# Experts 4 to 7 in one pass over all their rows, in a Mamba-2 and switch-routing kernel

## The chip, the cores and the metric

The kernel runs on one core of one Trainium2 chip. The metric is the device time of one execution in microseconds, and the median of several executions is compared. Beside it there is one execution that the hardware profiler recorded; all durations of single instructions come from that one.

A core has a matrix engine (PE, with PEld for its weight loads), a vector engine (DVE), a scalar engine (ACT), GpSimd (POOL) and a sync engine (SP), which here only issues transfers. Each engine works through its own list of instructions in order; semaphores tie the lists together.

## The reference, cut to what matters

Two blocks stand one behind the other. The first is a Mamba-2 state-space scan over 4 batches, 8 heads, 768 positions, head dimension 32 and state size 16. Its result is turned into 3072 rows of 256 numbers. The second sends each row to one of eight experts:

```python
logits = x @ w_gate                      # 3072 x 8
expert_idx = np.argmax(logits, axis=1)
probs = softmax(logits)                  # the reference writes it out
gate_w = probs[np.arange(N), expert_idx]
for e in range(E):
    mask = expert_idx == e
    xe = x[mask]
    h = np.maximum(xe @ w1[e], 0.0)      # 256 -> 1024
    out[mask] = gate_w[mask, None] * (h @ w2[e])   # 1024 -> 256
```

How many rows an expert gets is known only once the scan and the routing are done. With the inputs of the reference the eight counts are 372, 343, 418, 417, 336, 365, 415 and 406.

## The kernel before, in words

**Attention part (0 to 60 us).** The scan is done in 12 steps `d`, each of two blocks of 128 positions (24 blocks `n`). A step loads its blocks (`load`, L183; the loop asks for blocks 2d+6 and 2d+7, so two to three steps ahead), masks and scales them (`masked_C` on ACT, `scaled_x` mostly on POOL), multiplies on PE (`scores`, `y_own`, `y_old`), applies the mask on DVE (`weigh`), carries the state on (`state`, `faded`, `whole`), and turns the result into rows together with their eight logits (`rows`, `rows_out`, `logits_of`). The order of all instructions is written out by hand in the main loop (`manual_schedule`, from L714); no planner moves them. The states of steps 4 and later need decay totals, which PE writes to PSUM in `totals` and `take_totals` (L248) copies out: `et` by DVE, `ew` by ACT (L252).

**Routing.** Blocks are grouped (`RGS`); for each group `choose`, `rank` and `ranked` find for every row its place in a table `x_hbm` in device memory, where expert `e` owns a stretch of `NR` rows, and `place` (L430; the DMA is at L421) writes the 128 rows of a block there with one indirect DMA issued by POOL. A row is `W` = 336 numbers (1344 bytes): the values, the parts of the logits, and the number of the token. Places that no token takes must hold zeros and a token number outside the output. Before the change this is done in two ways: `empty_last` (L174) writes zeros over the last 64 rows of the first 256 of each expert, at step 1 of the loop, before any row is placed; and `empty_rest` (L473) writes 128 rows behind the last row of each expert, once the counts are known, with eight indirect DMAs during the expert part.

**Expert part (60 us to the end).** Each expert's rows are worked on in two passes: a first pass over 256 rows, expert after expert (`m_h` and `m_y`, loop at L869), and a second pass over what is left, two experts at a time (`m_pair`, L615). "Up" is the multiplication by `w1`: eight tiles of 128 hidden values, two matmuls each, with the rows of the expert as moving columns (`up`, L547), and ACT takes each result through Relu into `hT` (L560 in the first pass, L628 in the second). "Down" is the multiplication by `w2`: here the hidden values are the stationary side, 128 rows of the expert to a tile, with eight matmuls of 256 columns for each tile (`m_y`, L586). The result is scaled by the gate value (`put`, by ACT at L573 or DVE at L571) and scattered to the output by POOL (L564).

The second pass has rows that are not known when the program is built, so it is a `Switch`: `SIZES` holds 17 numbers of columns from 128 to 192 in steps of four, DVE computes for each pair of experts which of them is the smallest that holds its rows (`over`, L447), PE and ACT load that number (`number_of`, L607) and branch into the case that has been built for it. A case holds both experts' up matmuls and, if there are more than 128 rows, one shared tile in which each expert owns 64 partitions (`m_half`, L592). A hint to fetch the case is given earlier (`switch_hint`). The end of the program holds a general path that is taken only if the routing does not fit these sizes.

**Buffers and queues.** `m_load` (L479) reads the rows of a pass back from `x_hbm` on SP's queue; `m_xT` (L515) transposes them on DVE and computes the gate values, with an exponential on ACT in between. Three `hT` buffers of 256 columns are used in turn. Weights of an expert are two matrices of 1 MB, each loaded in four parts of 256 KB by `load_w` (L202) on SP's queue. Experts 0 to 2 have memory of their own from the start; those of 3 to 7 lie in memory that the attention part has given back. Which step of the loop loads which part of the first weights stands in `wq` (L751): four parts at step 0, one each at steps 1 to 8, and four at step 9; the rest of expert 2 follows at step 10. All these are behind each other on SP: a transfer that waits holds up those issued after it.

Of the kernel before, what the change touches and what calls it, by code (L numbers as in the profile page):

```python
# [9 lines left out]
FP32 = mybir.dt.float32  # L10
BF16 = mybir.dt.bfloat16
I32 = mybir.dt.int32
# [22 lines left out]
W = RW + 16  # L35
# [4 lines left out]
SLACK, FEW = 64, 64  # L40
NR = N + 512
# [6 lines left out]
def ssd_then_moe(ctx, tc, xs_in, ae_in, wgx, w_gate, w1, w2, gx, gb, gc, ga, out):  # L48
# [35 lines left out]
    rest = route.tile([128, E], I32, name="rest")  # L84
    at_r = route.tile([128, E], FP32, name="at_r")
# [5 lines left out]
    steps = route.tile([1, len(SIZES) - 1], FP32, name="steps")  # L91
# [69 lines left out]
    def empty_consts():  # L161
# [4 lines left out]
        at_i = sm.tile([128, E], I32, name="at_i")  # L166
        nc.gpsimd.iota(at_i, pattern=[[NR, E]], base=0, channel_multiplier=1)
        nc.gpsimd.tensor_copy(at_r, at_i)
        steps_i = sm.tile([1, len(SIZES) - 1], I32, name="steps_i")
        nc.gpsimd.iota(steps_i, pattern=[[SIZES[1] - SIZES[0], len(SIZES) - 1]], base=P1 + SIZES[0],  # L170
                       channel_multiplier=0)
        nc.gpsimd.tensor_copy(steps, steps_i)

    def empty_last():  # L174

        x_e = x_hbm.rearrange("(e r) w -> r e w", e=E)
        nc.sync.dma_start(out=x_e[P1 - SLACK:P1], in_=bc(zrows[0:SLACK, None, :], [SLACK, E, W]))
# [70 lines left out]
    def take_totals(w):  # L248
# [3 lines left out]
        nc.scalar.copy(ew[:, 12 * w:12 * w + 12], p)  # L252
# [194 lines left out]
    def over():  # L447
# [3 lines left out]
        nc.vector.tensor_tensor(out=rest, in0=p[:, 0:E], in1=at_r, op=ALU.add)  # L451
# [6 lines left out]
        nc.vector.tensor_tensor(out=over_, in0=bc(most[:, :, None], sh), in1=bc(steps[:, None, :], sh), op=ALU.is_gt)  # L458
# [14 lines left out]
    def empty_rest(e):  # L473
        to_places(zrows[:, :], rest[:, e:e + 1])

    jobs = [(0, e) for e in range(E)] + [(1, e) for e in range(E)]
    ex = [dict() for _ in jobs]

    def m_load(i, engs=(nc.sync,)):  # L479

        p, e = jobs[i]
        r0, n = e * NR + P1 * p, (P1, P2)[p]
        xb = mo.tile([128, P1 // 32 * 64], FP32, name="xb", bufs=4)
# [4 lines left out]
        lt = mo.tile([128, 2, MID], FP32, name="lt", bufs=7)[:, 0:2 - p]  # L488
        nc.sync.dma_start(out=lt, in_=x_hbm[r0:r0 + 128 * (2 - p), DM:W].rearrange("(t p) w -> p t w", p=128))
        ex[i]["lt"] = lt  # L490
        if p and e % 2 == 0:
            lh = mo.tile([128, 1, MID], FP32, name="lh", bufs=3)
            for u in range(2):
                q = r0 + u * NR + 128
                nc.sync.dma_start(out=lh[64 * u:64 * u + 64, 0], in_=x_hbm[q:q + 64, DM:W])
            ex[i]["lh"] = ex[i + 1]["lh"] = lh

    def gates(mid, n):

        sh = [128, n, E]  # L500
        l = mo.tile([128, 2, E], FP32, name="t_l", bufs=2)[:, 0:n]
        logits(l, mid)
        mx = mo.tile([128, 2], FP32, name="t_mx", bufs=2)[:, 0:n]
# [489 lines left out]
```

## Time and profile before

| | us |
|---|---|
| median of three executions | 254.2 (253.08 to 256.35) |
| the profiled execution, its own time | 247.47 |
| its span, first to last instruction | 245.8 |
| busy: PE, PEld, DVE, ACT, POOL | 237.3, 201.3, 88.5, 92.7, 82.8 |
| up matmuls (L551), busy, 512 records | 90.0 |
| down matmuls (L586), busy, 384 records | 85.1 |
| moved by DMA | 39.75 MB |

A record of a matmul is half of one: each multiplication of 32-bit numbers is two instructions here, so 256 matmuls are 512 records. The length given for a single record includes time in which the next one is already running, so paces are taken from the starts of long groups. In a timeline line the first number is the start in us from the beginning of the span, the second the length of the group, then come engine, line, operation, what is written and read, and shapes; a bracket at the end gives the idle time before the group and what ended it. `PEldq` and `ACTq` are the sequencers of PE and ACT, which handle branches themselves and can be ahead of their engines.

### The profile page before, as it was taken

Reading aid. Unit: us, or ns where it says so; the run is one execution under the profiler, and the core shown is the slowest. Engines: PE = TensorE matmul, PEld = TensorE weight load, DVE = VectorE, ACT = ScalarE, POOL = GpSimd, SP = SyncE. Lnnn points to the kernel's source line nnn. Section 1 sums busy time; section 2 is a strip of 40 time slices with the busy share of each in tenths; the row PEclk is TensorE's granted clock in tenths of the full one; section 3 lists DMA queues with packets and bytes.
Section 4 is the critical chain, followed back from the end, with each engine's and each line's share of the span. In section 5 each row is a group of like instructions: output and inputs, shape, how many; then the busy total and the mean of one; then the engine's idle time right before and its main releaser. Section 6 shows DMA issues by size and latency. Waiting matters only on the chain. (4 is left out here: it accounts for less than half of the span.)

```text
span 245.8 us, 5525 instructions
## 1 busy us (share of the span) xinstructions
PE 237.3 (97%) x2021; PEld 201.3 (82%) x2021; DVE 88.5 (36%) x279; ACT 92.7 (38%) x312; POOL 82.8 (34%) x144
## 2 busy tenths in 40 slices
PE   8889899999999999999999999999999999999992
PEld 5567778777888888888888888888999969989781
DVE  4699879998520222020201102052316007040000
ACT  4656768981322224141422324131432502614200
POOL 2484688880038506060413330111113012013031
PEclk9999999999999999999999999999999999999999
DMA  6999979965932278696867779454303100001001
GB/s 174 327 328 323 332 250 302 291 263 102 274 141 97 112 144 274 189 256 217 235 243 213 272 168 311 87 99 82 73 13 68 32 15 29 27 4 40 3 16 45
DMA packets 36407, 39.75 MB, mean 162 GB/s; under 512 B 21947, under 2 KB 23806, under 8 KB 36352
## 3 DMA queue, kind: packets, MB, share of 16 engines
q1 hardware_dynamic: 32816, 30.24, 43.2%
q0 software_dynamic: 2880, 8.66, 9.3%
q8 instruction: 27, 0.44, 0.7%
q10 hardware_dynamic: 656, 0.18, 0.3%
q14 instruction: 28, 0.23, 0.3%
HBM read 29.72 MB, written 9.86 MB: 161 GB/s over the span
## 5 line engine op out<-in xcount | busy, mean ns | idle before, releaser
L551 PE MATMUL h_ps<-xT,w 128*128 128x256 f32 (+3 forms) x512 | 90.0, 334 | 0.3 <-ACT hT L628 0.3
L551 PEld LDWEIGHTS h_ps<-xT,w 128*128 128x128 f32 x512 | 80.8, 190 | 7.6 <-ACT hT L628 0.7
L586 PE MATMUL y_ps<-w,hT 128*128 128x256 f32 x384 | 85.1, 380 | 0.0
L586 PEld LDWEIGHTS y_ps<-w,hT 128*128 128x128 f32 x384 | 72.6, 190 | 10.5 <-issue 0.8
L564 POOL DMA_INDIRECT out_dram<-yo,lt x24 | 23.8, 991 | 58.1 <-DVE yo L571 31.3
L509 DVE TENSOR_REDUCE t_se<-t_sub 128x1 f32<-128x8 f32 (+1 forms) x20 | 3.3, 165 | 102.8 <-ACT t_sub L507 102.8
L560 ACT ACTIVATE hT<-h_ps 128x256 f32<-128x256 f32 x64 | 24.4, 384 | 29.4 <-PE h_ps L551 28.9
L282 DVE TENSOR_TENSOR M<-g,mask 128x1024 f32<-128x1024 f32 x24 | 28.2, 1218 | 3.8 <-PE g L277 3.6
L628 ACT ACTIVATE hT<-h_ps 128x128 f32<-128x128 f32 (+2 forms) x64 | 18.0, 292 | 24.1 <-PE h_ps L551 24.1
L421 POOL DMA_INDIRECT x_hbm<-rows,pos x24 | 23.9, 994 | 9.3 <-DVE pos L408 5.3
L573 ACT ACTIVATE yo<-y_ps,t_gt 128x256 f32<-128x256 f32 x14 | 6.6, 474 | 43.2 <-PE y_ps L586 43.2
L421 POOL DMA_INDIRECT x_hbm<-zrows,rest x8 | 7.7, 962 | 35.4 <-DMA lt<-x_hbm 24.9
L335 PE MATMUL y<-M,xp 128*32 128x128 f32 x384 | 15.3, 277 | 1.6 <-DVE M L282 1.3
L347 PEld LDWEIGHTS r<-turn,yT 128*128 128x128 f32 x88 | 12.2, 189 | 4.4 <-ACT yT L340 3.0
L261 ACT ACTIVATE cm<-xs_n,par 128x128 f32<-128x128 f32 x46 | 15.1, 419 | 1.5 <-DMA xs_n<-in_xs_dram 1.5
L347 PE MATMUL r<-turn,yT 128*128 128x160 f32 x88 | 14.9, 312 | 0.7 <-ACT ew L252 0.7
L564 POOL DMA_INDIRECT out_dram<-yh,lh x4 | 3.9, 983 | 33.1 <-ACT yh L602 21.2
L277 PE MATMUL g<-cm,xs_n 32*128 32x256 f32 x192 | 15.0, 423 | 0.0
L271 POOL TENSOR_TENSOR xp<-xs_n,Ei 128x256 f32<-128x256 f32 x20 | 12.1, 617 | 6.8 <-DVE last L241 3.6
L571 DVE TENSOR_SCALAR yo<-y_ps,t_gt 128x256 f32<-128x256 f32 x10 | 4.7, 483 | 24.2 <-PE y_ps L586 24.2
L340 ACT COPY yT<-y 128x512 f32<-128x512 f32 x12 | 7.0, 586 | 16.1 <-PE y L335 14.2
L520 DVE STREAM_TRANSPOSE xT<-xb 128x512 f32<-128x512 f32 (+1 forms) x16 | 9.8, 632 | 8.6 <-DMA xb<-x_hbm 7.1
(123 smaller groups left out, 156.2 us busy)
## 6 DMA issues: line engine op xcount, KB each, us to landing
w<-in_w_dram SPq DMA_DIRECT2D x64, 256.0 KB, 5.8
xs_n<-in_xs_dram SPq DMA_DIRECT2D x20, 320.0 KB, 5.8
xb<-x_hbm SPq DMA_DIRECT2D x30, 64.0 KB, 2.3
xb<-x_hbm SPq DMA_DIRECT2D x32, 48.0 KB, 2.4
xs_n<-in_xs_dram SPq DMA_DIRECT2D x4, 192.0 KB, 3.6
x_hbm<-zrows SPq DMA_DIRECT2D x1, 672.0 KB
lt<-x_hbm SPq DMA_DIRECT2D x8, 80.0 KB, 2.7
xs_n<-in_xs_dram SPq DMA_DIRECT2D x4, 128.0 KB, 2.3
```

The costliest lines, as they stand in the source:

```text
L261: nc.scalar.mul(t[:, u], st[n]["CT"], par[:, u:u + 1])
L271: eng.tensor_tensor(out=t, in0=st[n]["x"].rearrange("p (h d) -> p h d", d=D), in1=bc(Ei[:, n, :, None], [128, NH, D]), op=ALU.mult)
L277: nc.tensor.matmul(g_ps[:, q, n % 2], lhsT=st[n]["BT"][r], rhs=st[n]["cm"][r].rearrange("p u i -> p (u i)"), start=True, stop=True)
L282: nc.vector.tensor_tensor(out=t, in0=g_ps[:, :, n % 2].rearrange("p q (u i) -> p q u i", u=2), in1=bc(mask[:, None, None, :], [128, 4, 2, ...
L335: nc.tensor.matmul(y_ps[o:o + D, h // 4, CH * s:CH * s + CH], lhsT=st[n]["xp"][:, D * h:D * h + D], rhs=st[n]["M"][:, h], start=first, sto ...
L347: nc.tensor.matmul((to[s] if to else r_ps[:, s])[:, 256 * t:256 * t + 160], lhsT=sd[d]["yT"][:, t, CH * s:CH * s + CH], rhs=turn[:, t].rea ...
L421: s_ = nc.gpsimd.indirect_dma_start(out=x_hbm[:, :], out_offset=bass.IndirectOffsetOnAxis(ap=at, axis=0), in_=row, in_offset=None)
L551: nc.tensor.matmul(p[:, 0:n], lhsT=w[:, c:c + 128], rhs=xT[:, t, 0:n], start=(t == 0), stop=(t == KT - 1))
L560: nc.scalar.activation(ex[i]["hT"][:, f, 0:n], q, func=ACT.Relu)
L564: return nc.gpsimd.indirect_dma_start(out=out[:, :], out_offset=bass.IndirectOffsetOnAxis(ap=tok, axis=0), in_=yo[:, :], in_offset=None, b ...
L586: nc.tensor.matmul(p, lhsT=ex[i]["hT"][:, f, 128 * t:128 * t + 128], rhs=w_sb[e][1][:, f * DM:f * DM + DM], start=(f == 0), stop=(f == FT ...
L628: nc.scalar.activation(ex[i + u]["hT"][:, f, 0:n], q, func=ACT.Relu)
```

## The change

Seven things are changed together:

- Experts 4 to 7 no longer have a first pass. They have one pass over all their rows, two experts at a time, in the same `m_pair`, with their own list of sizes, `WSIZES`: 17 numbers of columns from 320 to 448 in steps of eight. A case holds both experts' up matmuls over all columns; three tiles of 128 rows each follow in `m_y`, and the shared tile holds rows from 384 on. Experts 0 to 3 keep their two passes, and the first-pass loop runs over four experts instead of eight.
- `hT` buffers have 448 columns, and there are two instead of three. Their columns 320 to 384 are filled with zeros by POOL at step 1.
- The rows of a one-pass expert are loaded into buffers of their own (`xw`, `xTw`, two each); the small buffers `lt` are three tiles wide and six instead of seven.
- All places that may stay empty are written with zeros at step 1 (`empty_places`): rows 192 to 255 of experts 0 and 1, and rows 320 to 447 of all eight, in two DMAs. `empty_rest` and its eight indirect DMAs are gone.
- Weights: the part loaded at step 1 moves to step 2 and so on, and step 9 loads one part instead of four; the other matrix of expert 1 is loaded at step 10 with all of expert 2. Experts 6 and 7 use the memory of experts 0 and 1, and their sixteen parts are issued after the first pair.
- In `take_totals`, the copy of `ew` for the second half of the steps is done by DVE instead of ACT.
- The case numbers of two pairs are loaded at a time; within a pair's turn the transposition of the next pair now stands before the loads of later ones in the text (they are on different engines).

```diff
+HE = E // 2
+PASS = ((0, P1, 2), (P1, P2, 1), (0, P1 + P2, 3))
+WSIZES = list(range(P1 + FEW, P1 + P2 + 1, 8))
...
+        for hT in hT_all:
+            nc.gpsimd.memset(hT[:, :, WSIZES[0]:P1 + 128], 0.0)
...
-    def empty_last():
+    def empty_places():
         x_e = x_hbm.rearrange("(e r) w -> r e w", e=E)
-        nc.sync.dma_start(out=x_e[P1 - SLACK:P1], in_=bc(zrows[0:SLACK, None, :], [SLACK, E, W]))
+        for r, n, e in ((P1 - SLACK, SLACK, 2), (P1 + FEW, P2 - FEW, E)):
+            nc.sync.dma_start(out=x_e[r:r + n, 0:e], in_=bc(zrows[0:n, None, :], [n, e, W]))
...
-        nc.scalar.copy(ew[:, 12 * w:12 * w + 12], p)
+        (nc.vector.tensor_copy if w else nc.scalar.copy)(ew[:, 12 * w:12 * w + 12], p)
...
-    def empty_rest(e):
-        to_places(zrows[:, :], rest[:, e:e + 1])
-
-    jobs = [(0, e) for e in range(E)] + [(1, e) for e in range(E)]
+    jobs = [(p, e) for p in range(2) for e in range(HE)] + [(2, e) for e in range(HE, E)]
...
-    hT_all = [mo.tile([128, FT, P1], FP32, name=f"hT{k}") for k in range(3)]
+    hT_all = [mo.tile([128, FT, P1 + P2], FP32, name=f"hT{k}") for k in range(2)]
...
     def m_half(i, n, yo):
-        e = jobs[i][1]
+        p, e = jobs[i]
+        a = 128 * PASS[p][2]
+        n = max(0, n - a)
...
     def m_pair(i, pp):
...
-            n = SIZES[c]
+            n = (SIZES, WSIZES)[p - 1][c]
...
-        wq = [0, 0, 0, 0, 1, 2, 3, 4, 5, 6, 7, 8, 9, 9, 9, 9]
+        wq = [0, 0, 0, 0, 2, 3, 4, 5, 6, 7, 8, 9]
...
-                for k in range(8):
-                    load_w(2, *divmod(k, 4))
+                for k in range(12, 24):
+                    load_w(k // 8, k % 8 // 4, k % 4)
...
-        for e in range(EW, E):
+        for e in range(EW, E - 2):
             w_sb.append([w2pool.tile([128, KT * F], FP32, name=f"w{u + 1}_{e}") for u in range(2)])
+        w_sb.extend(w_sb[0:2])
...
-        for i in range(E):
+        for i in range(HE):
...
-                if 1 <= i <= 4:
-                    for e in range(2 * i - 2, 2 * i):
-                        empty_rest(e)
                 m_load(i + 3)
-                if i == E - 1:
+                if i == HE - 1:
                     m_load(i + 4)
...
         for k in range(E // 2):
-            i = E + 2 * k
+            i = HE + 2 * k
             m_pair(i, pp)
             if k + 1 < E // 2:
                 tc.switch_hint(chosen(k + 1), len(SIZES), f"pair{k + 1}")
+                m_xT(i + 2)
                 for u in range(4, 6):
                     if i + u < len(jobs):
                         m_load(i + u)
-                m_xT(i + 2)
             m_y(i, pp)
             m_y(i + 1, pp)
+            if k == 0:
+                for e in range(E - 2, E):
+                    for j in range(8):
+                        load_w(e, *divmod(j, 4))
```

## The prediction

> **What bounds the kernel now.** I read the page's busy shares first, then TensorE's timeline from 85 us on, then who waits on TensorE, then the other engines' timelines in the attention part, and last the branches at the four pairs. PE is busy for 97% of the span. The Trainium skill warns that busy time flatters a pipelined engine, so I took the pace from the timeline instead (start, length, what, count):
>
> ```profile
> PE 237.3 (97%) x2021; PEld 201.3 (82%) x2021; DVE 88.5 (36%) x279; ACT 92.7 (38%) x312; POOL 82.8 (34%) x144
> ...
> 152.23 7.07 PE L586 MATMUL y_ps<-w,hT 128*128 128x256 f32 x32
> 159.14 7.07 PE L551 MATMUL h_ps<-xT,w 128*128 128x256 f32 x32
> 166.04 7.07 PE L586 MATMUL y_ps<-w,hT 128*128 128x256 f32 x32
> 172.95 7.31 PE L551 MATMUL h_ps<-xT,w 128*128 128x128 f32 x64
> 180.09 7.07 PE L586 MATMUL y_ps<-w,hT 128*128 128x256 f32 x32
> 187.00 9.25 PE L551 MATMUL h_ps<-xT,w 128*128 128x164 f32 x64
> ...
> 206.78 7.31 PE L551 MATMUL h_ps<-xT,w 128*128 128x128 f32 x64
> 213.92 7.07 PE L586 MATMUL y_ps<-w,hT 128*128 128x256 f32 x32
> 220.83 2.34 PE L551 MATMUL h_ps<-xT,w 128*128 128x160 f32 x16
> 223.44 6.79 PE L551 MATMUL h_ps<-xT,w 128*128 128x160 f32 x48 [0.27 <-ACT hT L628]
> ```
>
> From 60 us to the end each group starts where the last one ends; the only gap is 0.27 us. So the expert part is TensorE's own stream, and only its length counts. A matmul is two records. The pace by start times: 256 columns, 6.907 us for 32 records, 215.8 ns each; 128 columns, 7.14 for 64, 111.6; 164 columns (187.00 to 196.19), 143.6; 160 columns (223.44 to 230.16 for 48), 140.0. That is 2n/2.4 plus 2.5 to 7 ns: time goes with columns, and a record has little cost of its own.
>
> The attention part (to 60 us) is a ring of DVE, PE and POOL: DVE is busy 8.3 to 9.5 of every 10 us, DMA at a share of 0.97 to 1.01 from 10 to 30 us, POOL 8.5 of 10 from 30 to 50 us.
>
> The third reading is the branch into a pair's case (duration min/median/max in ns, then its start):
>
> ```profile
> L988 PEldq COMPARE_BRANCH  x1: 343/343/343, 169.4 to 169.4; - x1
> ...
> L988 PEldq COMPARE_BRANCH  x1: 3072/3072/3072, 183.6 to 183.6; - x1
> ...
> L988 PEldq COMPARE_BRANCH  x1: 3295/3295/3295, 217.2 to 217.2; - x1
> ```
>
> Into case 0 (128 columns) the branch takes 0.3 us; into case 9 (164) and 8 (160) it takes 3.1 and 3.3. PE's sequencer reaches it 3.4 to 3.6 us before the array runs out of work (183.6 against 187.00, 217.2 against 220.83). The long branch is hidden with about 0.3 us to spare.
>
> **What the Trainium skill says.** "TensorE: Matmul & The Clock Gate", Back-to-back issue gap: warm, N/2.4 + 2.5 ns. With two passes to a record the trace agrees at 256 columns (213.3 + 2.5). "Runtime: NRT & Kernel Launch", Instruction fetch mechanics: a taken branch outside what is prefetched must fetch its page by DMA first; the 0.3 against 3.1 us agrees. "DMA: Bandwidth & Descriptors", Queues, rings and completion order: an engine takes its queues in turn, packet by packet, so a fetch shares with data; no run here shows that price. "Perfetto Trace Analysis", Identifying the Most-Contended Engine, is the warning used above.
>
> **The change, part by part.** The reference's routing counts are 372, 343, 418, 417, 336, 365, 415, 406 rows. Pairs (0,1) and (2,3) keep 128 and 164 columns. Pair (4,5) takes 368 columns (case 6), pair (6,7) 416 (case 12).
>
> 1. *One pass.* Pair (4,5) now: two first passes of 6.907 and 7.14 us, together 20.95. After: 64 records of 368 columns at 736/2.4 + 2.5 = 309.2 ns, 19.79. Gain 1.16. Pair (6,7) now: 13.81 + 9.06 (9.33 less the 0.27 gap) = 22.87; after, 416 columns, 349.2 ns, 22.35. Gain 0.52. The down matmuls stay: three tiles for each expert before and after, the 32-row half too. The 0.27 gap goes: it stands because ACT, late from its own branch (first eviction at 223.08), had four h_ps buffers of 0.56 us in hand; wide ones are 1.24 to 1.40 each, some 5 us of cover. Sum −1.95. Evictions fall from 128 to 64 for experts 4 to 7; by 0.83 ns per column ((384 − 278)/128) a 416-column one takes about 0.52 us against 1.40: hidden. Hidden-state buffers drop from 3 to 2; each is refilled only after the down matmuls that read it, which PE has behind it, so nothing.
>
> 2. *Branches.* Pair (4,5) goes from case 0 (0.3 us) to case 6: between 0.3 and 3.3 us, against a lead of 3.4 to 3.6: 0 to 0.2. Pair (6,7): the same, 0 to 0.2. Pair (2,3) keeps case 9, but its branch (about 128 to 131 us) now meets the weights of part 3. If sharing adds nothing it is free; if it doubles 3.1 us, 2.8 of it show. ACT's branch (186.3 to 188.9, 2.6 us) is late beside it, over a cover of 2.3, and overlaps. I take +0.9 for all branches, 0 to +3; a gain is excluded, as none costs PE time now.
>
> 3. *Weights moved back.* Experts 6 and 7 (16 loads, 4 MB) go into the memory of 0 and 1: SP waits for pair (0,1)'s down matmuls, about 131 us, with nothing behind it but loads 10 and 11, first needed about 171. At 256 KB per 0.7 us (370 GB/s, as at 10 to 14 us) the data are in by about 138, needed at 192. Four loads leave the attention part for the burst at 60.8 us (12 instead of 8): +2.8 us, in by about 72; the second matrix of expert 1 is used at 83, expert 2 at 90. Covered. The eight writes of empty rows (7.7 us of POOL, 27.7 us of waits of SP's x loads) go; those waits ended before any PE wait, so nothing is gained. The x loads for the first pair move up instead: by my count of SP's issues they land by about 107, when DVE wants them; a microsecond of lateness would only hold evictions that PE needs after 112.
>
> 4. *Empty places in step two.* 1152 rows of 1344 B in two DMAs instead of 512 rows in one: 0.86 MB more, less one weight load moved off. At the 211 to 343 GB/s seen from 16 to 22 us that is 2.5 to 4.1 us, less 0.7: what is queued behind, the xs_n loads issued at 16.5 and 17.2 (7.0 us to landing), comes 1.8 to 3.4 us later, from 23.5–24.2 to 25.3–27.6. ACT reads them from 24.86, is done 1.3 us later, and then has 1.82 us idle before 28.44: 0 to 0.7 of delay. POOL's first placement (23.04) waits for these writes and holds the sums of states and xp behind it; POOL's idle after it is 0.85, 1.29 and 0.60 us up to 35.2, and xp made at 26.7 is used at 32.4: about nothing. POOL's two added fills of hT (512 elements each; 336 took 0.37 us) cost about 1.1, covered by its 2.60 idle at 20.11; without that cover they would add as much.
>
> 5. *Copy by VectorE.* PE waits 0.67 us at 30.15 for ACT's ew copy (0.22 us at 29.88, behind yT, Er, Ei and S). On DVE it follows its neighbour at about 28.1, costs 0.17 to 0.2 there, before an idle 0.42. Gain up to 0.67 for PE; but the first expert starts when its rows are placed and read, and POOL, which places them, has only 0.28 + 0.21 of waits after 37 us to give up. Parts 4 and 5 together: −0.2, from −0.67 to +0.8.
>
> Sum: −1.95 + 0.9 − 0.2 = −1.25. The profiled execution took 247.47 us (span 245.8): 246.2. The median shown, 254.2, lies 6.7 above that execution; its three runs span 253.08 to 256.35. I carry the difference over: 253.0.
>
> **The rivals.**
> *A, the branch shows.* The fetch into pair (2,3)'s case shares DMA with 3 MB of weights, and the wide cases lie far off. For: 0.3 us to spare, and case 0 is left. Against: other busy stretches show no PE gap, though there nothing branches. With 3 us at pair (2,3) and 0.4 at the wide pairs: −1.95 + 3.4 − 0.2 = +1.3, 255.5, slower than before. It decides once the added branch time exceeds 2.15 us.
> *B, the empty rows reach PE.* If placement and xs_n come later than POOL's and ACT's slack, the attention part grows by 1.8 us: −1.95 + 0.9 + 1.8 = +0.75, 255.0. For: DMA at 1.0 there. Against: three idle stretches of POOL, and loads issued two steps ahead.
> *C, everything hidden.* No branch shows, and the copy gives its 0.67: −2.6, 251.6.
>
> **How the numbers follow.** Forecast 0.5, A 0.2, B 0.12, C 0.18. Range 250.6 (C less 1 for the spread of medians) to 256.4 (A plus 0.9). A measurement here tells about 2% from no change: 249.1 and 259.3. Beyond the first I see only luck, 0.05; beyond the second a branch or a queue far worse than seen, 0.08; within, 0.87.
>
> **What would show it.** Right: up-projection groups of 64 records spaced about 309 and 349 ns, no gap in them; no wait of PE for ew; the first placement near 25 us; the start of the first expert at 60.0 to 60.6. Branch entries of 3 us or more for the wide pairs, and a gap of PE near 131. Wrong if the wide records take more than columns tell, if PE waits for late rows near 60 us, or if a branch costs many microseconds.

## The result and the profile after

The change made the kernel slower. The median is 265.35 us (262.31 to 268.28, six executions) against 254.22 us (253.08 to 256.35, six executions of the kernel before beside them). The ratio is 1.037, with a 95% interval of 1.032 to 1.042. This ratio leaves out the two longest of the six executions after, 268.13 and 268.28 us, which are 2.2% and more above the shortest; the profiled one (span 266.6) is one of the two, so its two losses below are checked in a second profile.

The page of the kernel after: busy times, and further down the granted TensorE clock in 40 slices.

```profile
PE 245.2 (92%) x1893; PEld 191.8 (72%) x1893; DVE 88.2 (33%) x260; ACT 83.6 (31%) x267; POOL 75.1 (28%) x129
...
PE   7897999897999999993999489999999999999992
...
PEclk9999899997999999998699979999999999999998
```

PE has 128 records fewer and yet is busy for 8 us more. Two slices of PE stand out at 3 and 4 tenths, in the middle of a part that was without gaps before. The clock row has a 6 behind the first of them and a 7 behind the second: the granted clock fell there. The timeline of PE in that stretch (start, length, what, count, idle before and who ended it):

```profile
112.15 7.07 PE L554 MATMUL h_ps<-xT,w 128*128 128x256 f32 x32
119.06 2.32 PE L589 MATMUL y_ps<-w,hT 128*128 128x256 f32 x10
125.42 7.88 PE L589 MATMUL y_ps<-w,hT 128*128 128x256 f32 x22 [4.05 <-DMA w<-in_w_dram]
133.14 7.31 PE L554 MATMUL h_ps<-xT,w 128*128 128x128 f32 x64
140.29 7.07 PE L589 MATMUL y_ps<-w,hT 128*128 128x256 f32 x32
149.50 2.49 PE L554 MATMUL h_ps<-xT,w 128*128 128x164 f32 x16 [2.14 <-DVE yo L574]
154.28 8.62 PE L554 MATMUL h_ps<-xT,w 128*128 128x164 f32 x48 [2.29 <-ACT hT L633]
...
173.43 19.95 PE L554 MATMUL h_ps<-xTw,w 128*128 128x368 f32 x64
193.22 7.07 PE L589 MATMUL y_ps<-w,hT 128*128 128x256 f32 x32
200.77 14.08 PE L589 MATMUL y_ps<-w,hT 128*128 128x256 f32 x64 [0.48 <-DVE yo L574]
214.69 22.51 PE L554 MATMUL h_ps<-xTw,w 128*128 128x416 f32 x64
```

The wide passes are as computed: from 173.43 to 193.22 is 19.79 us for 64 records of 368 columns; from 214.69 to 237.13, where the next group starts, is 22.44. What was lost stands ahead of them. The down matmuls of expert 3 take from 119.06 to 133.14, 14.08 us where 32 such records took 6.907. And the up matmuls of pair (2,3) begin 2.14 us late and stop again for 2.29 us.

**The first loss.** The bracket names a weight transfer, but the weights of expert 3 had been read by ten records already. What was late are hidden values. The timelines of DVE and of ACT in the kernel after, one after the other:

```profile
120.91 0.58 DVE L523 STREAM_TRANSPOSE xT<-xb 128x384 f32<-128x384 f32 x1 [4.52 <-DMA xb<-x_hbm]
```

```profile
116.67 0.38 ACT L563 ACTIVATE hT<-h_ps 128x256 f32<-128x256 f32 x1 [0.48 <-PE h_ps L554]
122.08 0.21 ACT L509 ACTIVATE t_sub<-t_sub 128x8 f32<-128x8 f32 x1 [5.03 <-DVE t_sub L508]
...
125.00 0.91 ACT L563 ACTIVATE hT<-h_ps 128x256 f32<-128x256 f32 x3
```

ACT has the three gate exponentials of pair (0,1) in its queue ahead of the last three Relu results of expert 3. The exponentials wait for DVE, and DVE waits until 120.91 for the rows of expert 1's second pass. So the Relu results come at 125.00, and PE takes up its work 0.42 us later. The reason for the late rows is in SP's queue (start of a group of issues, its length, what is loaded, how many):

```profile
103.07 3.38 SPq L487 DMA_DIRECT2D xb<-x_hbm  x4
...
109.48 3.83 SPq L206 DMA_DIRECT2D w<-in_w_dram  x8
113.41 3.61 SPq L487 DMA_DIRECT2D xb<-x_hbm  x4
```

The rows of expert 0's second pass are asked for at 103.07. Those of expert 1 are asked for only at 113.41, behind 2 MB of weights of expert 4, which are not read before 173. Between the issues SP waits for earlier transfers (3.6 us in 5 waits of the row loads from 100 to 122 us); DMA is at a share of 0.85 to 1.06 from 112 to 122 us.

**The clock.** The 22 down records that would take 4.75 us at 215.8 ns each took 7.7 us (125.42 to 133.14). In stretches of 2 us (busy time and count of PE, PEld, DVE, ACT and POOL, then granted clock, DMA share, GB/s) the kernel after shows it:

```profile
122.00:124.00 2.00, 0.00 (x0) 0.00 (x0) 1.17 (x8) 0.42 (x2) 0.00 (x0) 1.00 0.87 222
124.00:126.00 2.00, 0.58 (x1) 0.50 (x2) 1.17 (x8) 1.03 (x4) 0.00 (x0) 0.61 0.89 276
126.00:128.00 2.00, 2.00 (x6) 1.63 (x5) 0.00 (x0) 0.00 (x0) 0.00 (x0) 0.50 1.04 295
128.00:130.00 2.00, 2.00 (x6) 1.55 (x6) 0.48 (x1) 0.00 (x0) 0.85 (x1) 0.50 0.38 66
130.00:132.00 2.00, 2.00 (x8) 1.65 (x7) 0.00 (x0) 0.00 (x0) 0.13 (x1) 0.68 0.52 132
132.00:134.00 2.00, 2.00 (x15) 1.84 (x14) 0.66 (x2) 0.21 (x1) 0.00 (x0) 1.00 0.45 90
```

After 4.05 us without work the granted clock is down to 0.50, and it is back at 1.00 from 132 us on. The wait and the slow records together cost 7.2 us (14.08 less 6.907).

**The second loss.** PE's sequencer at the choice of pair (2,3): the hint that announces the case, then the branch into it (duration three times in ns, start):

```profile
L924 PEldq BRANCH_PREFETCH_HINT  x1: 36/36/36, 139.9 to 139.9; - x1
...
L996 PEldq COMPARE_BRANCH  x1: 5750/5750/5750, 143.6 to 143.6; - x1
```

The branch takes 5.75 us instead of 3.07 in the profile before, and ends at 149.35; PE starts at 149.50. ACT's first result in that case is late too: ACT is idle for 6.58 us ahead of it (2.68 in the profile before), which gives the second stop.

### The profile page after: what moved, and what is told of

It reads as the page before. It is cut to its first block, busy times and chain, and to the rows that moved or that the text cites. A ratio compares the mean times of both kernels' runs of the same rounds, so it can differ in the third digit from the quotient of the medians.

```text
span 266.6 us, 5144 instructions
## 1 busy us (share of the span) xinstructions
PE 245.2 (92%) x1893; PEld 191.8 (72%) x1893; DVE 88.2 (33%) x260; ACT 83.6 (31%) x267; POOL 75.1 (28%) x129
## 5 line engine op out<-in xcount | busy, mean ns | idle before, releaser
L589 PE MATMUL y_ps<-w,hT 128*128 128x256 f32 x384 | 87.9, 389 | 4.5 <-DMA w<-in_w_dram 4.0
L554 PE MATMUL h_ps<-xT,w 128*128 128x256 f32 (+2 forms) x256 | 47.0, 344 | 4.4 <-ACT hT L633 2.3
L554 PEld LDWEIGHTS h_ps<-xT,w 128*128 128x128 f32 x256 | 42.0, 198 | 8.3 <-ACT hT L633 2.5
L633 ACT ACTIVATE hT<-h_ps 128x128 f32<-128x128 f32 (+3 forms) x64 | 24.9, 395 | 65.0 <-PE h_ps L554 58.3
L554 PE MATMUL h_ps<-xTw,w 128*128 128x368 f32 (+1 forms) x128 | 42.5, 492 | 0.0
L554 PEld LDWEIGHTS h_ps<-xTw,w 128*128 128x128 f32 x128 | 24.3, 190 | 17.4 <-issue 9.9
L574 DVE TENSOR_SCALAR yo<-y_ps,t_gt 128x256 f32<-128x256 f32 x18 | 8.4, 482 | 63.5 <-PE y_ps L589 63.5
L511 DVE TENSOR_REDUCE t_se<-t_sub 128x1 f32<-128x8 f32 (+2 forms) x16 | 2.7, 168 | 55.3 <-ACT t_sub L509 47.8
L563 ACT ACTIVATE hT<-h_ps 128x256 f32<-128x256 f32 x32 | 11.9, 382 | 16.8 <-PE h_ps L554 13.5
L279 PEld LDWEIGHTS g<-cm,xs_n 32*128 32x128 f32 x192 | 9.7, 194 | 5.7 <-issue 5.2
```

The costliest lines, as they stand in the source:

```text
L279: nc.tensor.matmul(g_ps[:, q, n % 2], lhsT=st[n]["BT"][r], rhs=st[n]["cm"][r].rearrange("p u i -> p (u i)"), start=True, stop=True)
L554: nc.tensor.matmul(p[:, 0:n], lhsT=w[:, c:c + 128], rhs=xT[:, t, 0:n], start=(t == 0), stop=(t == KT - 1))
L563: nc.scalar.activation(ex[i]["hT"][:, f, 0:n], q, func=ACT.Relu)
L589: nc.tensor.matmul(p, lhsT=ex[i]["hT"][:, f, 128 * t:128 * t + 128], rhs=w_sb[e][1][:, f * DM:f * DM + DM], start=(f == 0), stop=(f == FT ...
L633: nc.scalar.activation(ex[i + u]["hT"][:, f, 0:n], q, func=ACT.Relu)
```

## The experiments

Each ratio compares with executions of the kernel before on the same chip, beside the run. The chip isn't the same for all runs: the kernel before took 255.61 us beside the first four, 254.65 beside the next four (from `before_again` on), 254.9 beside the next four (from `before_loads` to `b_ew`), and 247.73 us beside the last four, so across these groups only ratios are compared.

**rows_first** has the row loads of a step ahead of its weight loads.

```diff
                 if f != FT // 2:
                     return
+                m_load(i + 3)
+                if i == HE - 1:
+                    m_load(i + 4)
                 if EW <= i + 2 < E - 2:
...
-                m_load(i + 3)
-                if i == HE - 1:
-                    m_load(i + 4)
```

> Theory 1: the changed kernel loses about 4 us where the second half of expert 3's down matmuls waits, because SP issues the rows of the first pair behind 2 MB of weights, so that the gate values, and behind them on ACT the last evictions of expert 3, come late. Issued ahead of the weights, the rows are there in time: the gap of 4.05 us in the down matmuls of expert 3 is gone, and the time falls by 3 to 5 us against the changed kernel (265.35), to about 261. Theory 2: the wait is for the weights themselves, as the label of the wait says; then the weights, now later still, make the gap longer, 5 us or more, and the time rises. Theory 3: the loss lies in the attention part alone; no change beyond 1 us.

Measured: 258.42 us, ratio 1.0113 (1.0033 to 1.0192). In SP's queue the rows of expert 1 now stand at 104.27:

```profile
104.27 4.27 SPq L487 DMA_DIRECT2D xb<-x_hbm  x4
...
110.26 3.99 SPq L206 DMA_DIRECT2D w<-in_w_dram  x8
```

and in PE's timeline the down matmuls of expert 3 are whole again:

```profile
116.59 7.09 PE L589 MATMUL y_ps<-w,hT 128*128 128x256 f32 x32
...
142.30 6.95 PE L554 MATMUL h_ps<-xT,w 128*128 128x164 f32 x48 [1.76 <-ACT hT L633]
...
160.81 20.02 PE L554 MATMUL h_ps<-xTw,w 128*128 128x368 f32 x64 [0.88 <-DVE t_se L511]
```

The order of two loads in one queue is worth 1.0368 − 1.0113 = 2.6%, 6.5 us, with an error of some 2 us; the forecast was 3 to 5. It isn't the rows alone: the branch into pair (2,3) fell with them, from 5.75 to 3.92 us, and that into pair (4,5) rose from 1.33 to 4.38. What is left shows at these two branches.

**w_late** issues the weights of experts 6 and 7 one pair later, so that they don't lie beside the branch of pair (2,3).

```diff
-            if k == 0:
+            if k == 1:
                 for e in range(E - 2, E):
                     for j in range(8):
                         load_w(e, *divmod(j, 4))
```

> The weights of experts 6 and 7 are issued after the second pair instead of the first. Theory 1: the branch into the second pair's case takes 5.75 us instead of 3.1 because its instructions are fetched beside these weights; without them it is back at 3.0 to 3.5 us, the gaps of 2.1 and 2.3 us of PE at the start of that pair fall to 0.3 or less, and the time falls by about 4 us, to about 261. The branch into the third pair may take over some of it, 0 to 2 us. Theory 2: the branch is long for the distance of its target or by chance; no change beyond 1 us, and a branch of 5 us or more stays.

Measured: 263.96 us, ratio 1.0315 (1.0236 to 1.0394). The stop in expert 3's down matmuls stays (4.29 us). The branch of pair (2,3) falls to 3.69 us, and its gap to 0.23 us. But the weights now meet the next branch, that of pair (4,5), which takes 5.21 us. PE's timeline:

```profile
124.16 6.42 PE L589 MATMUL y_ps<-w,hT 128*128 128x256 f32 x22 [4.29 <-ACT hT L563]
...
147.43 6.95 PE L554 MATMUL h_ps<-xT,w 128*128 128x164 f32 x48 [0.23 <-ACT hT L633]
...
166.83 5.18 PE L554 MATMUL h_ps<-xTw,w 128*128 128x368 f32 x16 [1.77 <-DVE t_se L511]
```

The stall moved with the weights. The 4 us forecast did not come: the ratio is 0.5% below that of the kernel after, less than its error.

**rows_first_w_late** has both edits.

```diff
+                m_load(i + 3)
+                if i == HE - 1:
+                    m_load(i + 4)
                 if EW <= i + 2 < E - 2:
...
-            if k == 0:
+            if k == 1:
```

> Both edits. Theory 1: the two gains add up, 7 to 9 us less than the changed kernel, about 257; PE has no gap above 0.5 us from the start of the first expert on. What is left against the kernel before then lies in the attention part: about 4 to 5 us. If instead one gap only hides the other, the gain is that of one edit, about 4 us.

Measured: 261.28 us, ratio 1.0231 (1.0148 to 1.0314), a miss. The branch of pair (4,5) took 6.18 us, the longest of all, at a DMA share of 0.96 to 1.05, and the wide pass behind it waited 2.68 us. The weights moved back only changed which branch pays.

**b_zeros** has part 4 of the change alone, in the kernel before.

```diff
-        nc.sync.dma_start(out=x_e[P1 - SLACK:P1], in_=bc(zrows[0:SLACK, None, :], [SLACK, E, W]))
+        for r, n, e in ((P1 - SLACK, SLACK, 2), (P1 + FEW, P2 - FEW, E)):
+            nc.sync.dma_start(out=x_e[r:r + n, 0:e], in_=bc(zrows[0:n, None, :], [n, e, W]))
...
-                if 1 <= i <= 4:
-                    for e in range(2 * i - 2, 2 * i):
-                        empty_rest(e)
```

> The kernel before with one part of the change: all places that may stay empty written at step 1, the eight later writes gone. Theory 1: about 0.9 MB more in the DMA-bound stretch from 16 to 24 us delays rows, placements and instruction fetches: 2 to 5 us slower than the kernel before, 256 to 259. Theory 2: these writes are hidden behind POOL's and ACT's idle time: within 1 us of 254.2.

Measured: 255.65 us, ratio 0.9989 (0.9964 to 1.0015). The added writes and the eight removed ones together change nothing that shows; they were not taken one by one.

**before_again** is the kernel before, unchanged, with a profile.

> The kernel before once more, for a second profile. The first profiled execution took 247.47 us, below all timed ones (254.0 and more). Theory 1: it was a lucky one; a usual execution starts the first expert near 67 us, not at 60.56, with the attention part held up by late instructions of PE, and runs the expert part in 185 us as before. Theory 2: the attention part is as short as shown, and the time above it lies outside the span or in the expert part.

Measured: 256.03 us, span 254.3. The first expert starts at 68.99 us in it and at 60.56 in the profile shown before; from there to the end the two agree within 1 us. In the profile after it starts at 68.93. These profiles show no loss in the attention part; that the two of the kernel before differ by 8 us says how little one profile tells there.

**quiet** is `rows_first` with the weights of experts 6 and 7 in the memory of experts 2 and 3 and those of expert 5 in that of expert 1, each loaded when its memory is free, so that none lies beside the branches of pairs (2,3) and (4,5).

```diff
-        for e in range(EW, E - 2):
+        for e in range(EW, E - 3):
...
-        w_sb.extend(w_sb[0:2])
+        w_sb.extend(w_sb[1:4])
...
-            if k == 0:
-                for e in range(E - 2, E):
-                    for j in range(8):
-                        load_w(e, *divmod(j, 4))
+            for e in ((5,), (7, 6), (), ())[k]:
+                for j in range(8):
+                    load_w(e, 1 - j // 4, j % 4)
```

> Rows ahead of weights, and no weight load near a branch: expert 5 uses the memory of expert 1, and experts 6 and 7 that of 2 and 3, each loaded only once the down matmuls before the branch are done. Theory 1 (a branch is slow while weights move): both long branches take 3.0 to 3.5 us, PE's gaps at the second and third pair fall to 0.3 us each, and the time is 2.5 to 3.5 us below the one with rows first (258.4): about 255.5. Theory 2 (distance or chance): branches of 4 us or more stay, and the time stays within 1 us of 258.4.

Measured: 254.7 us, ratio 1.0007 (0.9982 to 1.0032). The branches take 3.47 and 3.31 us. The loss is gone, and so is the gain: PE still waits 1.08 us in pair (2,3) and 0.58 us for a result buffer in pair (4,5).

**static_rows_first** and **static_before** leave out the choice of size in the second step of the work: only the case that these inputs need is built, so nothing is announced and nothing branched over. They compute the reference for these counts alone.

```diff
-        for c in tc.Switch(chosen(e // 2), len(SIZES), hint=f"pair{e // 2}"):
+        for c in [(0, 9, 6, 12)[e // 2]]:
...
-        tc.switch_hint(chosen(0), len(SIZES), "pair0")
...
-                tc.switch_hint(chosen(k + 1), len(SIZES), f"pair{k + 1}")
```

> Rows ahead of weights, and the choice of the size is left out: only the case that these inputs need is built for each pair, so no engine branches there. Theory 1: the branches and what they hold up cost 4 us in the kernel with rows first, so about 254; what is left is the gain of the one pass less a wait for a result buffer, and the time lies 1 to 2 us below the kernel before with its choice left out too. Theory 2: branches cost nothing, and the wide pass or the attention part is slower than argued: within 1 us of 258.4.

> The kernel before with the choice of the size left out in the same way. Its branches hide behind PE's queue but for 0.3 us: within 0.5 us of the kernel before, 255. It is the measure for the run above: the difference of the two is what the wide pass is worth without branches, 1 to 2 us by the count of columns.

Measured: 252.19 us, ratio 0.9889 (0.9815 to 0.9963), for `static_rows_first`; 253.73 us, 0.9966 (0.9937 to 0.9994), for `static_before` (cases 0, 9, 0, 8). Without branches the expert part of the first has no gap; PE's timeline:

```profile
138.66 9.07 PE L554 MATMUL h_ps<-xT,w 128*128 128x164 f32 x64
...
158.26 19.95 PE L554 MATMUL h_ps<-xTw,w 128*128 128x368 f32 x64
178.04 20.88 PE L589 MATMUL y_ps<-w,hT 128*128 128x256 f32 x96
```

So the choice of size costs 0.3% in the kernel before and 1.0113 − 0.9889 = 2.2% (5.7 us, with an error of almost 3) in `rows_first`. From the first expert on, the two profiles are 4.6 us apart (187.9 and 183.3). The one pass with its companions gains 0.9966 − 0.9889 = 0.8%, 2.0 us, and this difference carries an error of about 0.8% itself.

**before_loads** puts sixteen weight loads, whose data nothing reads, into the kernel before behind the first pair.

```diff
             m_y(i, pp)
             m_y(i + 1, pp)
+            if k == 0:
+                for e in range(2):
+                    for j in range(8):
+                        load_w(e, *divmod(j, 4))
```

> The kernel before, with one thing added: sixteen weight transfers of 0.5 MB each (8.4 MB), issued after the down matmuls of the first pair at the place where the kernel after issues those of experts 6 and 7. They go into the memory of experts 0 and 1, which nothing reads any more, so they carry no result and only load the DMA queues. Theory (the branch of the next pair is slow because its instructions are fetched beside the weights): the compare-and-branch of TensorE for pair (2,3) goes from 3.1 to 3.7 us to 5 us or more, PE waits 1.5 to 3 us more at that pair, and the time goes up by 1.5 to 4 us (255.7 to 258.2 against 254.2). Rival (the weights are harmless, and the stall at that pair belongs to the one-pass order of the kernel after): the branch stays within 3.1 to 3.7 us and the time within 0.6 us of before.

Measured: 256.66 us, ratio 1.0056 (1.0032 to 1.0079), 1.4 us slower: just under the 1.5 to 4 us of the theory, with a branch of 4.13 us, under its 5 (3.07 to 3.72 in the two profiles before):

```profile
L992 PEldq COMPARE_BRANCH  x1: 4127/4127/4127, 192.6 to 192.6; - x1
```

DMA traffic makes the branch longer, but not to 5.75 us here. (The expectation calls the sixteen loads 8.4 MB. They are of 256 KB each, 4.2 MB, as in the kernel after.)

**quiet_few** has half as many sizes.

```diff
-SIZES = list(range(128, P2 + 1, 4))
+SIZES = list(range(128, P2 + 1, 8))
...
-WSIZES = list(range(P1 + FEW, P1 + P2 + 1, 8))
+WSIZES = list(range(P1 + FEW, P1 + P2 + 1, 16))
```

> The kernel of run quiet, with half as many sizes for each pair: steps of 8 instead of 4 rows for the first four experts' second pass, of 16 instead of 8 for the one pass of the other four (9 cases each instead of 17, so the program has about half as many instructions behind each choice). Pair (2,3) takes 168 columns instead of 164 (64 records, two pieces of N/1.2 ns: 64 x 3.3 = +0.2 us), the wide pairs keep 368 and 416. Theory A (a branch is slow by the distance it has to fetch over): both slow branches, 3.47 and 3.31 us in quiet, fall by 1 us or more, and the time goes to 252.5 to 253.7. Theory B (a branch is slow whenever its target isn't yet fetched, whatever the distance): they stay at 3.2 to 3.6 us, the time stays at 254.5 to 255.

Measured: 255.68 us, ratio 1.0008 (0.9982 to 1.0034); branches of 3.85 and 3.78 us, no shorter than in `quiet`. Half the cases, and so a target about half as far, don't lower the price. The first case of all is another matter, as the readings under "The hint" show.

**b_wq** and **b_ew** are the weight order and the copy by VectorE, each alone in the kernel before.

```diff
-        wq = [0, 0, 0, 0, 1, 2, 3, 4, 5, 6, 7, 8, 9, 9, 9, 9]
+        wq = [0, 0, 0, 0, 2, 3, 4, 5, 6, 7, 8, 9]
...
-                for k in range(8):
-                    load_w(2, *divmod(k, 4))
+                for k in range(12, 24):
+                    load_w(k // 8, k % 8 // 4, k % 4)
```

> The kernel before, with the order of the weight transfers alone changed as in the kernel after: eight instead of twelve weight transfers are issued early beside the attention part, twelve instead of eight at its end. Theory: no change beyond 0.8 us, since the first expert's weights are in before 67 and the later transfers have 40 us of room. Rival (the weights moved back delay the first experts or the row loads already here): 1 to 3 us slower.

```diff
-        nc.scalar.copy(ew[:, 12 * w:12 * w + 12], p)
+        (nc.vector.tensor_copy if w else nc.scalar.copy)(ew[:, 12 * w:12 * w + 12], p)
```

> The kernel before, with one edit: the second of the two copies to the tile ew is made by VectorE instead of ScalarE. The prediction put this at up to 0.67 us faster. Theory: 0 to 0.7 us faster (253.5 to 254.2), as the copies stand in series ahead of the attention part. Rival: VectorE's own queue is what the start waits for, and nothing or up to 0.3 us is lost.

Measured: 255.02 us, ratio 1.0005 (0.998 to 1.003), and 253.84 us, ratio 0.9958 (0.9937 to 0.9978). The weight order alone is neutral. The copy gains 1.1 us (0.6 to 1.6), and the first expert starts at 67.28 us in its profile against 68.67 in that of `b_wq`. `b_ew` is the one version here with the choice of size that is faster than both kernels.

**The hint.** Read over all profiles, the branches show something else than distance: each is announced by a hint, and for all cases but the first the time from the hint to the end of the branch lies in one band. The last column is the mean DMA share over that time.

| run, pair | hint given | branch begins | lead | branch | hint to end | DMA share |
|---|---|---|---|---|---|---|
| profile before, (2,3) | 179.7 | 183.6 | 3.9 | 3.07 | 7.0 | 0.09 |
| profile before, (6,7) | 213.5 | 217.2 | 3.7 | 3.30 | 7.0 | 0.03 |
| after, (4,5) | 165.1 | 169.8 | 4.7 | 1.33 | 6.0 | 0.08 |
| quiet, (2,3) | 130.0 | 133.7 | 3.7 | 3.47 | 7.2 | 0.51 |
| before_loads, (2,3) | 188.9 | 192.6 | 3.7 | 4.13 | 7.8 | 0.68 |
| quiet, (4,5) | 150.0 | 155.0 | 5.0 | 3.31 | 8.3 | 0.34 |
| rows_first_w_late, (2,3) | 129.9 | 133.6 | 3.7 | 3.72 | 7.4 | 0.88 |
| rows_first, (4,5) | 151.4 | 156.2 | 4.8 | 4.38 | 9.2 | 0.87 |
| after, (2,3) | 139.9 | 143.6 | 3.7 | 5.75 | 9.5 | 0.92 |
| w_late, (4,5) | 156.5 | 161.4 | 4.9 | 5.21 | 10.1 | 0.95 |
| rows_first_w_late, (4,5) | 150.7 | 155.5 | 4.8 | 6.18 | 11.0 | 1.00 |
| after, (6,7) | 189.8 | 211.1 | 21.3 | 0.30 | | |
| profile before, (4,5), first case | 198.3 | 203.2 | 4.9 | 0.29 | 5.2 | 0.06 |
| rows_first, (0,1), first case | 114.3 | 119.9 | 5.6 | 0.35 | 6.0 | 0.88 |

Up to a share of 0.51 the band is 6.0 to 8.4 us, from 0.68 to 0.88 it is 7.4 to 9.2, above 0.9 it is 9.5 to 11.0 (with the branches not listed). Traffic orders it only roughly.

What moves in that time shows in the profile's DMA queues, two of which are named "instruction" (queue, packets, MB, share). In the profile before, from hint to end of the branch of pair (2,3) (179.7 to 186.7 us) and of pair (4,5) (198.3 to 203.5):

```profile
q8 instruction: 2, 0.03, 1.7%
...
q8 instruction: 1, 0.02, 1.5%
```

So it is in every profile with branches: two packets for a case other than the first, one or none for the first, whatever the traffic. In the profile before the two packets of pair (2,3) fall within 0 to 1.3 and 4.3 to 5.3 us after the hint; in the kernel after, beside the weights, within 1.1 to 2.1 and 6.1 to 7.1. For pair (6,7) in the kernel after both have moved by 194, 17 us ahead of the branch, which then takes 0.30 us. That the branch waits for these packets is read from their times; no run took them away alone.

The last four runs test this: lead against distance, and the share of each loss alone.

**after_again** is the kernel after with a second profile.

> The kernel after, unchanged, once more with a profile, since the profiled execution was the longest of six. If the theory is complete, a time of 262 to 266 us shows the same two places: the down matmuls of expert 3 take 12 to 14 us instead of 6.9, and the up matmuls of pair (2,3) wait 2 to 4.5 us. Rival (the profiled execution was disturbed): one of the two is missing, and the time is made up elsewhere.

Measured: 262.83 us, span 261.1, against 247.73 us for the kernel before on that chip. This single execution is 15.1 us slower, more than the 9.4 us of the ratio 1.037. From the first expert to the end it takes 197.9 us, as the first profile after (197.7), where both profiles before take 185.2 and 185.3. Both places are there, in PE's timeline:

```profile
120.39 7.14 PE L589 MATMUL y_ps<-w,hT 128*128 128x256 f32 x22 [4.62 <-ACT hT L563]
...
144.06 3.67 PE L554 MATMUL h_ps<-xT,w 128*128 128x164 f32 x16 [2.48 <-DVE yo L574]
148.79 8.52 PE L554 MATMUL h_ps<-xT,w 128*128 128x164 f32 x48 [1.05 <-ACT hT L633]
```

Here the releaser of the first stop is named as ACT's Relu, and the branch into pair (2,3) takes 6.09 us.

**static_after** is the kernel after without the choice of size (left out as in `static_rows_first`, with the same edit).

> The kernel after with the choice of size left out: only the sizes that these inputs need are built, nothing is branched over and no hint is given. Weights, rows and their order stay as in the kernel after. Theory (two causes that add up): the branch's share goes and the late rows stay, 258.5 to 260.5 us: from one side static_rows_first, 252.19, plus the 6.9 us between after and rows_first, from the other 265.35 less 4.4 to 6. The down matmuls of expert 3 still take 12 us or more. Rival (late rows and late branch are one thing, the branch being late because DVE and SP are): 252 to 255 us. Other rival (the branch is harmless): 264 to 266 us.

Measured: 251.49 us, ratio 1.0141 (1.0095 to 1.0188). The microseconds expected were for a chip with 254.2 us before; in ratios they are 1.017 to 1.025, and the rival with one cause in place of two was 0.991 to 1.003. The rest is a little smaller than the first theory had it, so two causes remain. PE's timeline keeps the first loss and has none at the pair:

```profile
109.71 2.32 PE L589 MATMUL y_ps<-w,hT 128*128 128x256 f32 x10
116.35 7.25 PE L589 MATMUL y_ps<-w,hT 128*128 128x256 f32 x22 [4.32 <-ACT hT L563]
123.44 7.31 PE L554 MATMUL h_ps<-xT,w 128*128 128x128 f32 x64
...
137.50 9.07 PE L554 MATMUL h_ps<-xT,w 128*128 128x164 f32 x64
```

**quiet_late_y** and **b_ew_late_y** move the down matmuls of the last first-pass expert behind those of the first pair, between the hint and the branch of pair (2,3). In `quiet_late_y` a third `hT` buffer is needed.

```diff
+        hT_all.append(w2pool.tile([128, FT, P1 + P2], FP32, name="hT2"))
+        nc.gpsimd.memset(hT_all[2][:, :, WSIZES[0]:P1 + 128], 0.0)
...
-        m_y(HE - 1, pp)
         for k in range(E // 2):
...
             m_y(i, pp)
             m_y(i + 1, pp)
+            if k == 0:
+                m_y(HE - 1, pp)
```

> The kernel of run quiet with the down matmuls of expert 3 moved behind those of the first pair (a third buffer for the hidden states, in memory that quiet leaves free, makes it possible). The hint for pair (2,3) is given as before, right behind the first pair, and now 7 us more of matmuls stand between it and the branch: a lead of some 10.6 us instead of 3.7. Theory (the prefetch needs 7 to 8 us from the hint, so lead is what counts): TensorE's branch into pair (2,3) falls from 3.5 us to about 0.3 us, its 1.1 us gap goes, and the time goes from 254.7 to 253 to 254. The branch into the wide pair (4,5), whose lead stays 4.7 us, stays at about 3.3 us. Rival (a far case costs 3 to 4 us whenever it is taken): both branches stay above 3 us and the time at 254.5 to 255.

> The kernel of run b_ew (before with the copy by VectorE) with the down matmuls of expert 7 moved behind those of the first pair in the same way; its three buffers for hidden states allow it as they are. Lead theory: the branch into pair (2,3) falls from 3.5 to about 0.3 us, the branch into pair (6,7) stays above 3 us, and the time, 253.84 in b_ew, falls by 0 to 0.6 us, since PE's queue hides most of a 3.5 us branch here. Rival: both branches stay, and the time with them.

Measured: 248.92 us, ratio 1.0038 (1.0012 to 1.0064), and 248.6 us, ratio 1.0015 (0.9988 to 1.0043). On the branch the theory holds: with a lead of 11.7 us (hint at 119.8, branch at 131.5) it takes 0.30 us in `quiet_late_y`,

```profile
L998 PEldq COMPARE_BRANCH  x1: 302/302/302, 131.5 to 131.5; - x1
```

and 0.29 us in `b_ew_late_y` (lead 11.2), while the branch of pair (6,7) there, with 3.7 us of lead, stays at 3.44. The branch of pair (4,5) in `quiet_late_y` was to stay at about 3.3 us and took 1.73, with 4.8 us of lead; why is not shown. On the time the theory misses, since the new order makes two waits of its own; PE's timeline in `quiet_late_y`:

```profile
113.29 6.96 PE L554 MATMUL h_ps<-xT,w 128*128 128x128 f32 x60 [1.47 <-ACT hT L563]
...
128.10 7.17 PE L589 MATMUL y_ps<-w,hT 128*128 128x256 f32 x32 [0.94 <-DVE yo L574]
```

Two groups of up matmuls behind each other outrun ACT, and three groups of down matmuls outrun the result buffers. 2.4 us of new waits stand against the 1.1 us that went.

## Why the prediction was wrong

It forecast 253.0 us, from a sum of −1.25 us; the median is 265.35. The runs divide the difference. Late rows: `static_after` less `static_rows_first`, 1.0141 − 0.9889 = 2.5%, 6.4 us of 254.2 (and 6.5 from the pair with branches). Branches: after less `static_after`, 1.0368 − 1.0141 = 2.3%, 5.8 us, less the 0.9 us that they cost before, so 4.9. One pass, zeros and copy together: −2.0. The sum is +9.3, and the ratio 1.0368 is +9.4 (the medians, which hold all executions, are 11.1 apart); since each term is a difference of the same few ratios, they must add up to it, and that proves nothing. Each term has an error of about 2 us. A second reading comes from the profiles, from the first expert to the end: 197.7 us after, 190.1 in `static_after`, 183.3 in `static_rows_first`, 184.6 in `static_before`, 185.2 before. It gives 6.8 us for the late rows, 7.0 for the branches and −1.3 for the one pass, 12.5 in all. So the rows come out alike, the branches between 5 and 7 us; the two profiled executions after lose some 3 us more than the ratio has, and why is open.

- **Step 1, one pass: right.** Predicted 19.79 and 22.35 us for the wide groups, measured 19.79 and 22.44. Against the profile before that is a gain of 1.9 us, forecast at 1.95; without branches it is 1.3 (`static_rows_first` against `static_before`), since 0.5 of it stood at the branch of pair (6,7). The wait for ACT in the last pair is gone. "Hidden-state buffers drop from 3 to 2 … so nothing" holds too: `static_rows_first`, with two, shows no gap there. With branches the step missed a small wait for a result buffer behind the first wide group (0.48 us at 200.77).
- **Step 2, branches: the mechanism right, the size wrong, so this step failed too.** The step took +0.9 from a range of 0 to +3; the term measured +4.9, beyond the range. The step asked how long a fetch takes when it shares with weights, and doubled 3.1 us at the worst. But 3.1 us was only the rest of a fetch that the hint had begun 3.9 us earlier; the whole is 7.0. A transfer that takes 9.5 instead of 7.0 puts all 2.5 us of the difference into the branch, since the lead stays (139.9 to 149.35, against 179.7 to 186.7). The step also counted PE's branch only: behind it the first result of ACT came late, another 1 to 2.3 us. The Trainium skill, "Runtime: NRT & Kernel Launch", Instruction fetch mechanics, says that a branch whose target isn't yet there waits for a fetch by DMA; the traces agree (two instruction packets for a case other than the first), and with the lead long enough the wait is gone (0.30 us).
- **Step 3, weights moved back: this is the step that failed most.** It put the late rows at nothing; they cost about 6.4 us. It said of the rows of the first pair "by my count of SP's issues they land by about 107 … a microsecond of lateness would only hold evictions that PE needs after 112". They were transposed at 120.91 in a profile whose attention part was 8.4 us later, so at 112.5 by the clock of the profile before, some 5 us later than counted. The terms of that count are not on record; what the trace has in those 5 us is that SP, behind the 2 MB of weights of expert 4, waits for earlier transfers to end. And the step did not follow the lateness through ACT's queue: the exponentials stand ahead of Relu results that PE needs at once. That the weights taken out of the attention part do no harm in the burst behind it was right (`b_wq`, 1.0005).
- **Step 4, empty places: right.** 0 to 0.7 us predicted for the writes and nothing gained by those removed; `b_zeros` measured 0.9989 for both together.
- **Step 5, the copy: its sign right, its size too small.** With step 4 it was entered at −0.2; alone it gave −1.1 (−0.6 to −1.6), an interval that holds the 0.67 that the step allowed at most.
- **The base.** Carrying the difference between the profiled execution and the median over was right: `before_again` has its 8 us more in the attention part, ahead of all that the losses touch.

Rival A had the branch of pair (2,3), but at +1.3 in all, and alone it would not have reached the time. No rival had the late rows. Of the prediction's own signs, "a gap of PE near 131" came true, at 147 to 154, which is 131 moved by the 8.4 us of the attention part and the 7.2 us of the first loss. Its sign of being wrong, a branch that costs many microseconds, came too (5.75); late rows came as well, but near 121 us and not near 60. The sign of branches of 3 us or more into the wide pairs did not come: 1.33 and 0.30 us.

Open is why the same 4.2 MB lengthen the branch to 5.75 us in the kernel after and only to 4.13 us in `before_loads`. From hint to end the DMA share is 0.84 to 1.02 in the one; in the other it is 0.28 from 190 to 192 us and 0.69 to 0.95 around it, so the fetch met less traffic. Whether that is the whole difference was not tried. Nor was it tried to take the exponentials out of the way of the Relu results with the rows left late.

## What to carry to other kernels

Where a queue is shared, order the loads by when their data are read: rows that were needed at once stood behind weights needed 60 us later, and that alone cost about 6 us. When a step is moved forward, follow the lateness through every in-order queue to the next instruction that PE needs, and price a stop of a little over 4 us as 6 to 7, since the clock falls. A branch over cases is priced from its hint, not from its own length: it cost nothing here when 11 us of work lay between them or when it went into the first case, and building only the needed case tells what it costs.

## What the runs showed of the hardware that was not expected

- From the hint to the end of the branch into a case other than the first took 6.0 to 8.4 us at a DMA share up to 0.51 and 9.5 to 11.0 us above 0.9; the branch itself takes 0.3 us when the lead is 11 us or more. Two instruction packets (0.03 MB) move in that time, one or none for the first case, whose branch took 0.29 to 0.35 us with 4.8 to 5.7 us of lead.
- In four profiles a stop of PE of 4.05 to 4.62 us brought the granted clock to 0.50; the 22 records behind it took 6.3 to 7.7 us instead of 4.75, and the group as a whole lost 6.0 to 7.2 us. After the stop of 2.68 us in `rows_first_w_late` the clock fell to 0.50 as well; after those of 1.76 and 1.77 us in `rows_first` and `w_late` the next groups show no slow records.
- The kernel before took 247.73 us on one chip and 254.65 to 255.61 on three others. The runs on the quick chip start their first expert at 59.48 to 63.19 us, those on the others at 65.7 to 69.6; the two profiles after, which start at 68.93 and 63.19, take 197.7 and 197.9 us from there on.
